# A fused adaLN attention and MLP block: weight loads queued behind the first keys' stores, key block loads between them, and one accumulator in another PSUM bank

## The chip, the core and the metric

The kernel runs on one core of a Trainium2 chip. The metric is device time in microseconds (us) of one launch. The engines that matter here are TensorE (PE, matrix products into the eight PSUM banks), VectorE (DVE), ScalarE (ACT), GpSimd (POOL) and SyncE (SP), which issues all of the DMA transfers in one queue, in program order. Each engine executes its own instructions in order; a semaphore makes one wait for another.

## What is computed

```
h  = layernorm(x) * (1 + ca) + sa                 # x: 2048 x 512
q, k, v = split(h @ wqkv)                          # 32 heads of width 16
o  = softmax(q k^T / 4) v                          # full attention, 2048 keys
x  = x + ga * (o @ wo)
h  = layernorm(x) * (1 + cb) + sb
x  = x + gb * (mish(h @ w1 + b1) @ w2)             # 512 -> 1792 -> 512
# sa, ca, ga, sb, cb, gb = silu(c) @ w_mod, in six parts of 512
```

All of it is fp32. The products are made at the fast rate of a rounded format: each operand is split into a high part and a low part, and three products (high-high, high-low, low-high) are summed in PSUM.

## The kernel before

The order of nearly all work is written out by hand. The program has four stages.

**Start** (lines 337 to 555). x and the first weight slices come in, the layer norm and its transposes are made per block of 512 rows (`tb` = 0 to 3), and the first unit of keys is made for each block, with the first unit of queries beside block 0. Such a unit (`qk_unit`) is 12 products of 128x512 into one PSUM bank; ACT rounds the bank to `qh`, DVE subtracts to `ql` (line 95), and SP stores both to the scratch tensor `kscr` in HBM (lines 284 and 285). From there `load_k` (line 330) loads the block back, 16 rows a head spread to three 16-row groups, into `ka0` and `ka1`, the two key tiles of the first head group. A bank is either one of the ring (`ring`, six banks, four in this stage) or one of the two separate banks `ms` and `acc`.

**Lead-in** (steps t = -20 to -1). Softmax needs the row maximum first. `max_pair` (line 587) makes two products of queries and keys into two neighbouring ring banks (line 595), and DVE reduces the pair to its maxima (line 597); there are 40 pairs, 32 of the first head group (`n` = 0: eight for each of the four key blocks, block by block), and 8 of the second. Beside each pair three or four slots of dense work run on PE (line 133): the rest of the q, k and v units, in *couples* of accumulators in the banks `ring` 4, `ring` 5, `ms` and `acc` in turn. When such a unit is finished, ACT copies its bank away (line 270 for queries and keys as `qf`, line 299 for values as `vq`), and for `qf` POOL makes `qh` and `ql`.

The units use weight slices. The list `plan` names them: its entry 0 is a unit of queries, entry 1 the value units, entries 2 and 3 key units. A slice comes by one DMA into the tile `wr` (line 233; there is one buffer), ACT rounds it to `wh` (line 88), and POOL subtracts to `wl` (line 95), which frees `wr`. The slice of entry i + 3 is loaded after the last unit of entry i, at a *hook*: `at(h, f)` runs f at half step h = 2t, so h fixes the place in the program and not a time.

In the same stage the first six of 32 weight blocks of the later MLP are prepared (`early_prep`, line 1565): a load of 256 KB into the tile `ep` (line 1570), a split on POOL (lines 92 and 95, seven half steps later), and two stores to `w1scr` (line 1578, three half steps after that). They start at the half steps -37, -34, ..., -22.

**Attention with the MLP beside it** (t = 0 to 511). Each step makes scores, their exponentials on ACT (line 639), the product with v (line 654), and the maxima of the head group after next (lines 581 and 583). The MLP of a finished block of rows runs in the gaps of PE.

**Tail.** The last block's output projection and MLP.

The maxima of the first head group must be in the query tiles before the first scores: `neg_max` (line 605), `max_rows` (line 614, a transpose on PE at line 616, then `mh` on ACT and `mt` on DVE), and four small DMAs `qa<-mt` (line 625).

DMAs are counted on eight semaphores in turn, so a DMA isn't issued before the eighth one ahead of it has landed.

Of the kernel before, what the change touches and what calls it, by code (L numbers as in the profile page):

```python
# [18 lines left out]
def adaln_block(ctx: ExitStack, tc: tile.TileContext, x, wqkv, wo, w1, b1, w2, c, w_mod, out):  # L19
# [9 lines left out]
    NB = S // TB  # L29
# [9 lines left out]
    PRO = 16 + LEAD  # L39
# [4 lines left out]
    LATE_LOAD = {4: -4, 5: 9}  # L44
# [41 lines left out]
    def hi_copy(eng, hi, src):  # L86
        if eng == "a":
            nc.scalar.copy(hi, src)
        elif eng == "v":
            nc.vector.tensor_copy(hi, src)  # L90
        else:
            nc.gpsimd.tensor_scalar(hi, src, 1.0, 0.0, op0=ALU.mult, op1=ALU.add)

    def lo_sub(eng, lo, src, hi):
        (nc.gpsimd if eng == "p" else nc.vector).tensor_sub(lo, src, hi.bitcast(F32))  # L95
# [15 lines left out]
    def mm3(acc, ah, al, bh, bl, late="a"):  # L111

        n = len(ah)
        seq = ((ah, bh), (ah, bl), (al, bh)) if late == "a" else ((ah, bh), (al, bh), (ah, bl))
        seq = [(l[k], r[k]) for l, r in seq for k in range(n)]
        for i, (l, r) in enumerate(seq):
            mm(acc, l, r, i == 0, i == len(seq) - 1)
# [42 lines left out]
    def bank(tag="ms"):  # L160
        if not isinstance(tag, str):
            return tag
        return ring() if tag == "ring" else ps.tile([P, TB], F32, tag=tag, name="bk", bufs=1)
# [39 lines left out]
    def at(h, f):  # L203

        hooks.setdefault(h, []).append(f)
# [23 lines left out]
    def slice_load(kind, i, pool=None, lp=None):  # L229
        w = P if kind < 2 else 2 * P  # L230
        raw = (pool or qp).tile([P, DK, w], F32, tag="raw" if pool is pw else "wr", name="wr", bufs=2 if lp else 1)
        o = kind * D + i * w
        nc.sync.dma_start(raw, wqkv[:, o:o + w].rearrange("(k p) m -> p k m", p=P))
        slices[kind, i] = raw
# [10 lines left out]
    def qk_unit(kind, ct, tb, tag):  # L245

        wh, wl = slices[kind, ct]
        acc = bank(tag)
        ts_ = slice(tb * TB, (tb + 1) * TB)
        mm3(acc, [wh[:, k, :] for k in range(DK)], [wl[:, k, :] for k in range(DK)],  # L250
            [h_h[:, k, ts_] for k in range(DK)], [h_l[:, k, ts_] for k in range(DK)], "b")

        def fin(h=None):
            late = h is not None and -4 <= h < 3
            if late and not spares:
                for v in range(2):
                    both = ap.tile([P, DK, TB], F32R, tag=f"o_{v}", name="late", bufs=1)
                    spares.extend(both[:, i, :] for i in range(DK))
            if late:
                qh, ql = spares.pop(), spares.pop()  # L260
            else:
                qh = qp.tile([P, TB], F32R, tag="qh", name="qh", bufs=2)
                ql = qp.tile([P, TB], F32R, tag="ql", name="ql", bufs=2)
            if h is None:
                hi_copy("a", qh, acc)
                lo_sub("v", ql, acc, qh)
            else:
                qf = (ap.tile([P, TB], F32, tag=f"p{len(spares) // 2 % 2 * 2}", name="qf", bufs=3) if late else
                      pw.tile([P, TB], F32, tag="raw", name="qf", bufs=1))
                nc.scalar.copy(qf, acc)  # L270
                hi_copy("p", qh, qf)
                lo_sub("p", ql, qf, qh)
            scr, rows = (qscr, 50) if kind == 0 else (kscr, 48)

            def put():
                put_away.add((kind, ct, tb))
                o = 8 * ct * rows * S + tb * TB
                if kind == 0:
                    for r, src in enumerate((qh, qh, ql)):
                        nc.sync.dma_start(dap(scr, o + r * S, [[rows * S, 8], [3 * S, DH], [1, TB]]), src.bitcast(F32))  # L280
                    return
                hi = qh.bitcast(F32)
                twice = bass.AP(tensor=hi.tensor, offset=hi.offset, ap=[list(hi.ap)[0], [0, 2], [1, TB]])
                nc.sync.dma_start(dap(scr, o, [[3 * S, P], [2 * S, 2], [1, TB]]), twice)
                nc.sync.dma_start(dap(scr, o + S, [[3 * S, P], [1, TB]]), ql.bitcast(F32))

            put() if h is None else at(clear(h + (5 if h > 60 else 2)), put)
        return fin
# [34 lines left out]
    def load_k(pp, tb=None):  # L323
        n, j = divmod(pp, 2)
        h = 4 * (n % G) + 2 * j
        kt = ka[pp % NR].bitcast(F32)
        at_ = slice(0, S) if tb is None else slice(tb * TB, (tb + 1) * TB)
        assert {(1, h // 8, i) for i in (range(NB) if tb is None else (tb,))} <= put_away, (pp, put_away)
        for s in range(2):
            nc.sync.dma_start(kt[64 * s:64 * s + 48, at_], kscr[h + s, :, at_])  # L330
# [6 lines left out]
    with ExitStack() as es:  # L337
# [185 lines left out]
        for tb in range(NB):  # L523
            if tb + 2 < NB:
                stats_tb(tb + 2)
            parts = []
            early = []
            for kind in (1, 0) if tb == 0 else (1,):
                fin = qk_unit(kind, 0, tb, "ring")
                parts.append((pe_queue[2 * DK:], fin))  # L530
                early.append(pe_queue[:2 * DK])
                pe_queue.clear()
            if tb == 0:
                (kw, qw) = early
                early = [[m for k in range(DK) for m in (kw[k], qw[k], kw[DK + k])], qw[DK:]]
            pe_queue.extend(m for e in early for m in e)
            pe_run()
            if tb in (1, 2):
                for kc in (2 * tb - 2, 2 * tb - 1):
                    unit(v_unit(0, kc, "ring"))  # L540
            if tb + 1 < NB:
                tr_tb(tb + 1, CUT1)
            for late, fin in parts:
                pe_queue.extend(late)
                unit(fin)
            if tb + 1 < NB:
                tr_tb(tb + 1, CUT2)
            if tb + 2 < NB:
                apply_tb(tb + 2)
            if tb == 0:  # L550
                for pp in range(2):
                    load_q(pp, 48)
            for pp in range(2):
                load_k(pp, tb)
        slice_split(0, 1)


# [534 lines left out]
    _, w1s, w2s, wos = state[last]  # L1092
# [407 lines left out]
    def do_specials(h):  # L1500
        if specials and h >= specials[0][0]():
# [5 lines left out]
    plan = [(-PRO, 0, 1, (0,)), (-PRO, 2, 0, range(4, 16)), (-PRO, 1, 1, range(NB)), (-PRO, 1, 2, range(NB)),  # L1507
            (-PRO, 0, 2, (0,)), (0, 2, 1, range(16)), (0, 1, 3, range(NB)), (0, 0, 3, (0,))]
# [3 lines left out]
    def planned(i, a, tag):  # L1512
        _, kind, sl, args = plan[i]
        unit = v_unit(sl, a, tag) if kind == 2 else qk_unit(kind, sl, a, tag)

        def fin(h):
            if a == args[-1]:
                if i + 2 < len(plan):
                    d = 4 if h > 0 else 1
                    split_at[i + 2] = LATE_SPLIT.get(i + 2, h + d)  # L1520
                    split = lambda: slice_split(*plan[i + 2][1:3], hi_eng="p" if h > 0 else "a")
                    split() if h < -4 else at(split_at[i + 2], split)
                if i + 3 < len(plan):
                    at(LATE_LOAD.get(i + 3, h + 7), lambda: slice_load(*plan[i + 3][1:3]))
            unit(h)
            if (kind, sl, a) == (2, 0, NKC - 1):
                at(max(0, h + 2), lambda: first_mods(max(0, h + 2)))
            if i + 1 == len(plan) and a == args[-1]:
                mst["qkv"] = h // 2 + 3
        return fin  # L1530

    at(-2 * PRO, lambda: slice_load(*plan[2][1:3]))
    order = (3, 4, 2, 5)

    def first_mods(h, j=0):
# [26 lines left out]

    EARLY = 6

    def early_prep(i, h):

        scr, src, _ = preps[i]
        lo, hi = [ap.tile([P, TB], F32R, tag=f"p{(1, 3, 0, 2)[i % 4]}", name="ep", bufs=4 - i % 4 // 2) for _ in range(2)]
        raw = lo.bitcast(F32)
        nc.sync.dma_start(raw.rearrange("p (k m) -> p k m", m=P), src)  # L1570

        def split():
            hi_copy("p", hi, raw)
            lo_sub("p", lo, raw, hi)

        def put():
            for v, part in enumerate((hi, lo)):
                nc.sync.dma_start(scr[:, v, :], part.bitcast(F32))

        at(h + 7, split)  # L1580
        at(h + 10, put)

    for i in range(EARLY):
        at(3 * i - 37, lambda i=i: early_prep(i, 3 * i - 37))

    def start_preps(h, i=EARLY, turn=0, puts=()):

# [75 lines left out]
```

## Time and profile before

| | |
|---|---|
| median of 3 runs | 1693.15 us (1690.56, 1694.89, 1693.15) |
| the profiled execution | 1691.93 us |
| its span, first to last instruction | 1690.1 us |
| mean granted TensorE clock | 0.996 of full speed |
| DVE busy over the span | 1431.6 us (85%) |
| ACT busy over the span | 1357.3 us (80%) |
| POOL busy over the span | 812.5 us (48%) |
| moved by DMA | 239.02 MB, mean 141 GB/s |

A busy time is the sum over an engine's instructions in the named stretch. In the time line a row gives start, duration, engine, line, operation, output and inputs, and in brackets the idle time just before it on its engine with what ended that. In the table by stretches a row gives busy time and instruction count of PE, of its weight loads, DVE, ACT and POOL, then the granted TensorE clock (1.00 is full speed), the busy share of the DMA engines and what they moved. All that the change touches lies in the first 104 us, the start and the lead-in.

### The profile page before, as it was taken

To read this page: it belongs to the slowest core of one execution; us is meant where nothing else is said; L and a number is where in the kernel's file an instruction comes from. 1 tells how busy PE (TensorE), PEld (TensorE's weight loads), DVE (VectorE), ACT (ScalarE), POOL (GpSimd) and SP (SyncE) were. 2 spreads that over 40 slices of the span, in tenths; PEclk is the share of its full clock that TensorE was granted. 3 is DMA by queue.
4 is the path that set the end of the run, shared out by engine and by line. 5 is a ranking of instruction groups with operands and counts; after the bars stand their busy time and mean duration, and the time that the engine had idled before them with its cause. 6 is when DMAs were issued, how large, how long until landed. Compare 5 with 4: busy or idle time off the path is not lost.

```text
span 1690.1 us, 34360 instructions
## 1 busy us (share of the span) xinstructions
PE 1667.0 (99%) x12707; PEld 932.1 (55%) x12707; DVE 1431.6 (85%) x2372; ACT 1357.3 (80%) x2618; POOL 812.5 (48%) x839
## 2 busy tenths in 40 slices
PE   8989999999999999999999999999999999999999
PEld 6855665555444455555555455555555455555687
DVE  6978888888989888888889888888889888883377
ACT  7157777777778988888888998888888998889674
POOL 5556224655313564556323565556323565555442
PEclk9999999999999999999999999999999999999999
DMA  7777556777755433434355434534354433534161
GB/s 261 218 272 200 147 147 188 222 222 216 230 146 143 113 95 93 121 88 129 85 137 152 115 77 93 141 76 126 87 145 122 130 94 81 144 103 131 76 228 63
DMA packets 114984, 239.02 MB, mean 141 GB/s; under 512 B 24500, under 2 KB 50120, under 8 KB 108864
## 3 DMA queue, kind: packets, MB, share of 16 engines
q1 hardware_dynamic: 114808, 236.82, 49.5%
q8 instruction: 100, 1.64, 0.4%
q14 instruction: 68, 0.56, 0.1%
q10 hardware_dynamic: 8, 0.00, 0.0%
HBM read 180.48 MB, written 51.45 MB: 137 GB/s over the span
## 4 chain that ended last, share of the span: by engine, by line
PE 89%; DVE 4%; DMA 3%; ACT 2%; issue 1%; SPq 0%; POOL 0%; ACTq 0%; DVEq 0%; POOLq 0%
PE bk L654 29%; PE ring L636 22%; PE ring L581 19%; PE bk L133 11%; PE ring L1267 2%; PE ring L126 2%; DVE mx L583 2%; ACT pr L639 1%; PE bk L126 1%; DVE mx L597 1%; PE ring L133 1%; DMA ka<-kscr 1%; DMA kscr<-qh 0%; DMA qa<-mt 0%; PE ring L970 0%
## 5 line engine op out<-in xcount | busy, mean ns | idle before, releaser
L583 DVE TENSOR_REDUCE mx<-ring 128x1 f32<-128x512 f32 x1968 | 1221.9, 681 | 151.1 <-PE ring L581 136.6
L639 ACT ACTIVATE pr<-ring 128x512 f32<-128x512 f32 x2048 | 1078.5, 603 | 207.5 <-PE bk L133 122.7
L581 PE MATMUL ring<-ka,qa 64*128 64x512 f32 x1968 | 817.8, 429 | 1.2 <-ACT pr L639 1.0
L636 PE MATMUL ring<-qa,ka 64*128 64x512 f32 x2048 | 759.1, 402 | 3.4 <-ACT pr L639 1.9
L654 PE MATMUL bk<-pr,vg 128*32 128x512 f32 x4096 | 545.1, 604 | 0.0
L581 PEld LDWEIGHTS ring<-ka,qa 64*128 64x128 f32 x1968 | 350.6, 184 | 326.2 <-DVE mx L583 251.4
L636 PEld LDWEIGHTS ring<-qa,ka 64*128 64x128 f32 x2048 | 373.8, 184 | 192.3 <-DVE mx L583 113.2
L133 PE MATMUL bk<-h,w 64*128 64x512 f32 (+1 forms) x1080 | 277.9, 390 | 0.0
L133 PE MATMUL bk<-w,a_h 64*128 64x512 f32 x632 | 211.1, 413 | 0.0
L133 PEld LDWEIGHTS bk<-h,w 64*128 64x128 f32 x1080 | 178.6, 185 | 10.0 <-ACT pr L639 1.5
L654 PEld LDWEIGHTS bk<-pr,vg 128*32 128x32 f32 x4096 | 81.3, 108 | 135.6 <-issue 126.4
L133 PE MATMUL bk<-w,a_l 64*128 64x512 f32 x316 | 124.3, 393 | 0.0
L133 PEld LDWEIGHTS bk<-w,a_h 64*128 64x128 f32 x632 | 106.8, 184 | 3.0 <-ACT hb L848 0.8
L1026 POOL TENSOR_TENSOR y<-yd,y 128x512 f32<-128x512 f32 x44 | 56.9, 1292 | 88.9 <-ACT yd L1025 79.5
L860 POOL TENSOR_SCALAR qq<-ee 128x512 f32<-128x512 f32 x25 | 15.5, 621 | 169.1 <-ACT ee L854 169.1
L876 POOL TENSOR_TENSOR qq<-qq,rr 128x512 f32<-128x512 f32 x42 | 54.2, 1289 | 85.7 <-ACT rr L870 85.7
L862 POOL TENSOR_TENSOR hb<-hb,ee 128x512 f32<-128x512 f32 x42 | 54.1, 1288 | 79.7 <-DVE ee L858 77.7
L133 PE MATMUL bk<-w,o_hl 64*128 64x512 f32 x288 | 79.3, 405 | 0.0
L95 POOL TENSOR_TENSOR a_l<-hb,a_h 128x512 fp32r<-128x512 f32 x53 | 73.1, 1379 | 4.4
L133 PE MATMUL bk<-h_h,wl 64*128 64x512 f32 x192 | 63.3, 426 | 0.3 <-ACT pr L639 0.3
L133 PEld LDWEIGHTS bk<-w,a_l 64*128 64x128 f32 x316 | 58.3, 185 | 3.1
L133 PE MATMUL bk<-h_h,wh 64*128 64x512 f32 x192 | 53.9, 413 | 5.1 <-ACT vq L299 4.8
(226 smaller groups left out, 1902.6 us busy)
## 6 DMA issues: line engine op xcount, KB each, us to landing
ka<-kscr SPq DMA_DIRECT2D x124, 384.0 KB
w<-w2scr SPq DMA_DIRECT2D x56, 512.0 KB
w<-w1scr SPq DMA_DIRECT2D x46, 512.0 KB
vg<-vscr SPq DMA_DIRECT2D x32, 552.0 KB
qa<-qscr SPq DMA_DIRECT2D x124, 100.0 KB
qscr<-qh SPq DMA_DIRECT2D x32, 256.0 KB
w2scr<-hl SPq DMA_DIRECT2D x14, 512.0 KB
kscr<-qh SPq DMA_DIRECT2D x12, 512.0 KB
```

Of the source, the lines that this page charges most:

```text
L95: (nc.gpsimd if eng == "p" else nc.vector).tensor_sub(lo, src, hi.bitcast(F32))
L126: nc.tensor.matmul(acc, l, r, start=start, stop=stop)
L133: i = nc.tensor.matmul(acc, l[64 * g:64 * g + 64], r[64 * g:64 * g + 64], start=start and not then, stop=bool(stop and then))
L581: nc.tensor.matmul(pm, qt[64 * s:64 * s + 64, qs * P:(qs + 1) * P], kt[64 * s:64 * s + 64, kb * TB:(kb + 1) * TB], start=True, stop=True)
L583: nc.vector.tensor_reduce(out=mxs[n][:, s, 4 * j + qs, kb:kb + 1], in_=pm, op=ALU.max, axis=AX.X)
L636: nc.tensor.matmul(p_, kt[64 * s:64 * s + 64, kc * P:(kc + 1) * P], qt[64 * s:64 * s + 64, :], start=True, stop=True)
L639: e = nc.scalar.activation(pr, p_, AF.Exp, scale=SCALE)
L654: nc.tensor.matmul(accs[n][32 * h:32 * h + 32, :], vgs[n][:, o:o + 32], pts.pop((t, h)), start=(kc == 0), stop=(kc == 15))
L862: (nc.vector if tail else nc.gpsimd).tensor_mul(hb, hb, ee)
L876: nc.gpsimd.tensor_mul(qq, qq, rr)
L1026: nc.gpsimd.tensor_add(y[i], yd, y[i])
L1267: nc.tensor.matmul(po[i // 2][:, i % 2, :], l[:, s], w[:, r, :], start=(f == 0 and j == 0), stop=(f == FT - 1 and j == 2))
```

## The change

The change has three parts. The loads of six MLP blocks are taken out of `early_prep` and put into `first_loads`, which runs at the first half step of the lead-in, together with the load of the slice of entry 2; their splits and stores get places of their own. The loads of key blocks 2 and 3 leave the start and go between those loads. The unit of keys of the last block (`tb` = 3) is summed in the bank `ms`. Besides, a slice that follows a unit finished before half step -20 (entry 3 alone) is loaded two half steps after that unit, where it was seven.

```diff
             for kind in (1, 0) if tb == 0 else (1,):
-                fin = qk_unit(kind, 0, tb, "ring")
+                fin = qk_unit(kind, 0, tb, "ring" if tb + 1 < NB else "ms")
...
             for pp in range(2):
-                load_k(pp, tb)
+                if tb < 2:
+                    load_k(pp, tb)
...
-                    at(LATE_LOAD.get(i + 3, h + 7), lambda: slice_load(*plan[i + 3][1:3]))
+                    at(h + 2 if h < -20 else LATE_LOAD.get(i + 3, h + 7), lambda: slice_load(*plan[i + 3][1:3]))
...
-    at(-2 * PRO, lambda: slice_load(*plan[2][1:3]))
+    def first_loads():
+        slice_load(*plan[2][1:3])
+        for i in range(EARLY):
+            early_load(i)
+            if i % 2:
+                for pp in range(2):
+                    if i < 4:
+                        load_k(pp, 2 + i // 2)
+
+    at(-2 * PRO, first_loads)
...
-    def early_prep(i, h):
+    raws = {}
+
+    def early_load(i):
 
         scr, src, _ = preps[i]
         lo, hi = [ap.tile([P, TB], F32R, tag=f"p{(1, 3, 0, 2)[i % 4]}", name="ep", bufs=4 - i % 4 // 2) for _ in range(2)]
         raw = lo.bitcast(F32)
         nc.sync.dma_start(raw.rearrange("p (k m) -> p k m", m=P), src)
+        raws[i] = scr, raw, hi, lo
+
+    def early_prep(i, h):
...
-        at(h + 7, split)
-        at(h + 10, put)
+        at(h, split)
+        at(h + 3, put)
 
     for i in range(EARLY):
-        at(3 * i - 37, lambda i=i: early_prep(i, 3 * i - 37))
+        early_prep(i, (-38, -36, -34, -32, -27, -25)[i])
```

The lines behind the first edit have other numbers in the changed program: 1570 is 1582, 1578 is 1595, 561 is 562, 595 is 596.

On SP, at the end of the start, the program before has, from the stores of key block 2 on (`kscr<-qh` and `kscr<-ql` are the stores of a key block, `ka_98` and `ka_99` the two key tiles of the first head group, `ep` the MLP blocks):

```order
L284 DMA kscr<-qh 128x2x512
L285 DMA kscr<-ql 128x512
L330 DMA ka_98<-kscr 48x512 x2
L330 DMA ka_99<-kscr 48x512 x2
L284 DMA kscr<-qh 128x2x512
L285 DMA kscr<-ql 128x512
L330 DMA ka_98<-kscr 48x512 x2
L330 DMA ka_99<-kscr 48x512 x2
L233 DMA wr<-in_A_wqkv 128x4x128
L1570 DMA ep<-in_B_w 128x4x128 x4
L1578 DMA w1scr<-ep 128x512 x2
```

and the changed program, from the same stores on:

```order
L284 DMA kscr<-qh 128x2x512
L285 DMA kscr<-ql 128x512
L284 DMA kscr<-qh 128x2x512
L285 DMA kscr<-ql 128x512
L233 DMA wr<-in_A_wqkv 128x4x128
L1582 DMA ep<-in_B_w 128x4x128 x2
L330 DMA ka_98<-kscr 48x512 x2
L330 DMA ka_99<-kscr 48x512 x2
L1582 DMA ep<-in_B_w 128x4x128 x2
L330 DMA ka_98<-kscr 48x512 x2
L330 DMA ka_99<-kscr 48x512 x2
L1582 DMA ep<-in_B_w 128x4x128 x2
```

The stores of key block 3 and the slice of entry 2 no longer stand behind the loads of key block 2, and all six `ep` loads stand ahead of the first store to `w1scr`.

On SP, a little later, around the load of the slice of entry 3 (the `wr` row; `qscr<-qh` and `qscr<-ql` store the query unit of entry 0, `vscr<-vq` values, `qa_102` and `ka_700` belong to the second head group), before:

```order
L280 DMA qscr<-ql 8x16x512
L1570 DMA ep<-in_B_w 128x4x128
L1578 DMA w1scr<-ep 128x512 x2
L306 DMA vscr<-vq 128x4x272
L1570 DMA ep<-in_B_w 128x4x128
L321 DMA qa_102<-qscr 50x512 x2
L330 DMA ka_700<-kscr 48x2048 x2
L1578 DMA w1scr<-ep 128x512 x2
L233 DMA wr<-in_A_wqkv 128x4x128
L1578 DMA w1scr<-ep 128x512 x4
```

and in the changed program (the tile `ka_700` is called `ka_693` there):

```order
L1595 DMA w1scr<-ep 128x512 x8
L233 DMA wr<-in_A_wqkv 128x4x128
L280 DMA qscr<-qh 8x16x512 x2
L280 DMA qscr<-ql 8x16x512
L1595 DMA w1scr<-ep 128x512 x2
L306 DMA vscr<-vq 128x4x272
L1595 DMA w1scr<-ep 128x512 x2
L321 DMA qa_102<-qscr 50x512 x2
L330 DMA ka_693<-kscr 48x2048 x2
```

The slice of entry 3 is now ahead of the query unit's stores, of the first value store of the lead-in and of the second head group's loads, and behind eight stores to `w1scr`.

On POOL the splits of the blocks (`ep`) and of the slice of entry 2 (`wl`) stand like this before:

```order
L561 MEMSET ka_702 128x2048
L92 TENSOR_SCALAR ep<-ep 128x512
L95 TENSOR_TENSOR ep<-ep 128x512
L95 TENSOR_TENSOR wl<-wr,wh 128x512
L92 TENSOR_SCALAR qh<-qf 128x512
L95 TENSOR_TENSOR ql<-qf,qh 128x512
```

and in the changed program:

```order
L562 MEMSET ka_695 128x2048
L92 TENSOR_SCALAR ep<-ep 128x512
L95 TENSOR_TENSOR ep<-ep 128x512
L92 TENSOR_SCALAR ep<-ep 128x512
L95 TENSOR_TENSOR ep<-ep 128x512
L92 TENSOR_SCALAR ep<-ep 128x512
L95 TENSOR_TENSOR ep<-ep 128x512
L92 TENSOR_SCALAR ep<-ep 128x512
L95 TENSOR_TENSOR ep<-ep 128x512
L95 TENSOR_TENSOR wl<-wr,wh 128x512
L92 TENSOR_SCALAR qh<-qf 128x512
L95 TENSOR_TENSOR ql<-qf,qh 128x512
```

The slice's split stands behind four block splits, where it stood behind one. PE, DVE and ACT keep their order; there only the bank of one key unit is another.

More of the change, by code (lines that the diff above doesn't have):

```diff
@@ L1570, in early_prep @@
         nc.sync.dma_start(raw.rearrange("p (k m) -> p k m", m=P), src)
+        raws[i] = scr, raw, hi, lo
+    def early_prep(i, h):
         def split():
+            scr, raw, hi, lo = raws[i]
             hi_copy("p", hi, raw)
@@ L1576, in put @@
         def put():
+            scr, _, hi, lo = raws.pop(i)
             for v, part in enumerate((hi, lo)):
                 nc.sync.dma_start(scr[:, v, :], part.bitcast(F32))
-        at(h + 7, split)
-        at(h + 10, put)
+        at(h, split)
+        at(h + 3, put)
     for i in range(EARLY):
-        at(3 * i - 37, lambda i=i: early_prep(i, 3 * i - 37))
+        early_prep(i, (-38, -36, -34, -32, -27, -25)[i])
     def start_preps(h, i=EARLY, turn=0, puts=()):
```

## The prediction

> **What bounds the kernel now.** I began with the table of stretches, because the share over the whole span hides where PE waits.
>
> ```profile
> 46.00:48.00 2.00, 0.84 (x3) 0.37 (x2) 0.75 (x2) 0.92 (x2) 0.16 (x1) 1.00 0.84 281
> 50.00:52.00 2.00, 2.00 (x16) 2.00 (x15) 1.51 (x2) 0.00 (x0) 2.00 (x2) 0.50 0.35 131
> 84.00:88.60 4.60, 0.00 (x0) 0.00 (x0) 1.35 (x2) 0.88 (x3) 0.18 (x1) 0.76 1.05 361
> 88.60:93.20 4.60, 4.53 (x21) 3.49 (x23) 1.80 (x4) 0.66 (x3) 2.95 (x3) 0.50 1.10 393
> 110.00:1690.00 1580.00, 1570.79 (x11876) 852.18 (x11875) 1345.02 (x2249) 1308.92 (x2534) 754.95 (x753) 1.00 0.48 133
> ```
>
> From 110 us to the end PE is busy 1570.79 of 1580 us, DVE 1345 and ACT 1309. The change moves nothing there, so what the lead-in gains or loses goes through to the end one for one. In the lead-in there are two holes: PE is busy 0.84 of 2 us at 46 to 48, and not at all from 84 to 88.6. After each the granted clock is down to 0.50. The time line of DVE shows what the holes cost, since DVE's 40 pair reductions set the pace between them.
>
> ```profile
> 47.70 0.69 DVE L95 TENSOR_TENSOR ql<-ring,qh 128x512 fp32r<-128x512 f32 x1 [1.25 <-ACT qh L88]
> 49.06 1.23 DVE L597 TENSOR_REDUCE mx<-ring 128x2 f32<-128x1024 f32 x1 [0.67 <-PE ring L595]
> 50.77 1.23 DVE L597 TENSOR_REDUCE mx<-ring 128x2 f32<-128x1024 f32 x1 [0.48 <-PE ring L595]
> 52.46 32.89 DVE L597 TENSOR_REDUCE mx<-ring 128x2 f32<-128x1024 f32 x29 [0.47 <-PE ring L595]
> 91.26 1.23 DVE L597 TENSOR_REDUCE mx<-ring 128x2 f32<-128x1024 f32 x1 [5.91 <-PE ring L595]
> 92.52 0.34 DVE L610 TENSOR_REDUCE mm<-mx 128x16 f32<-128x64 f32 x2
> 92.97 2.42 DVE L597 TENSOR_REDUCE mx<-ring 128x2 f32<-128x1024 f32 x2
> 95.30 0.33 DVE L619 SCALAR_TENSOR_TENSOR mt<-mh,lows,ring 32x128 fp32r<-32x128 f32 x1
> 95.99 7.01 DVE L597 TENSOR_REDUCE mx<-ring 128x2 f32<-128x1024 f32 x6 [0.35 <-PE ring L595]
> ```
>
> 29 reductions run without a gap in 32.89 us, 1.134 us each. DVE is idle for 0.67, 0.48, 0.47 and 5.91 us, each time for PE. The waits and the rows of PE and ACT say why PE was late:
>
> ```profile
> ACT wh L88 <- DMA wr<-in_A_wqkv: 7.1, 1, 7.1
> PE bk L133 <- ACT vq L299: 4.8, 1, 4.8
> 46.22 0.78 PE L126 MATMUL ring<-h_l,wh 128*128 128x512 f32 x2 [0.16 <-POOL h_l L479]
> 48.44 0.58 PE L595 MATMUL ring<-ka,qa 64*128 64x512 f32 x2 [1.44 <-DVE ql L95]
> 103.05 0.49 PE L636 MATMUL ring<-qa,ka 64*128 64x512 f32 x1 [0.43 <-DVE mx L597]
> 80.25 0.37 ACT L299 COPY vq<-bk 128x256 f32<-128x256 f32 x1 [2.32 <-PE bk L133]
> 87.72 0.62 ACT L88 CAST wh<-wr 128x512 fp32r<-128x512 f32 x1 [7.10 <-DMA wr<-in_A_wqkv]
> 88.25 0.37 ACT L299 COPY vq<-bk 128x256 f32<-128x256 f32 x1
> ```
>
> At 84 us PE needs the accumulator that ACT empties at 88.25. ACT had been ready since 80.62, but the rounding of the weight slice of entry 3 stands ahead of that copy, and the slice landed only at 87.7. At 47 us the first pair waits for `ql`, because the last key unit sits in a ring bank that the pair needs. At 103.05 the first scores of attention wait for DVE: the lead-in ends when its reductions end.
>
> **The change, part by part.** *The bank.* With the unit in `ms`, the first pair no longer waits for `ql`. PE can issue it when its last unit product has been issued, two products of about 0.22 us after 46.22, at 46.7 instead of 48.44. DVE still makes `ql` first, until 48.39, so the first reduction starts there and not at 49.06: 0.67 us. The unit itself must now wait until `ms` is free of the last transposes. DVE's row for that bank, before the unit's fourth product waits for ACT anyway, is
>
> ```profile
> 42.31 0.75 DVE L474 SCALAR_TENSOR_TENSOR hf<-bk,modc,h_h 128x512 f32<-128x512 f32 x1
> 44.16 0.50 PE L126 MATMUL ring<-h_h,wh 128*128 128x512 f32 x1 [0.18 <-ACT h_h L473]
> ```
>
> so three products start at 43.06 and are through by 43.7, before the fourth can start at 44.16. It costs nothing; without that cover it would be 0.3 us.
>
> *The idle times behind the first two reductions* (0.48 and 0.47) come from a PE at half clock: the first three reductions start 1.71 and 1.69 us apart, since the pairs come no faster. PE now leads by two pairs when DVE starts, so both idle times go, 0.95 us, if the clock holds. Bounds 0 and 0.95; I take 0.95, with the other end as a rival.
>
> *The slice of entry 3.* When is it issued and when needed? SP and POOL rows of before:
>
> ```profile
> 46.97 0.98 SPq L285 DMA_DIRECT2D kscr<-ql  x1
> 51.33 1.71 SPq L330 DMA_DIRECT2D ka<-kscr  x4
> 59.61 2.09 SPq L1570 DMA_DIRECT2D ep<-in_B_w  x4
> 73.75 0.80 SPq L1570 DMA_DIRECT2D ep<-in_B_w  x1
> 76.38 0.78 SPq L330 DMA_DIRECT2D ka<-kscr  x2
> 79.00 0.38 SPq L233 DMA_DIRECT2D wr<-in_A_wqkv  x1
> 49.48 5.29 POOL L561 MEMSET ka<- 128x2048 f32 x3
> 63.42 0.63 POOL L92 TENSOR_SCALAR ep<-ep 128x512 fp32r<-128x512 f32 x1 [8.65 <-DMA ep<-in_B_w]
> 65.37 1.29 POOL L95 TENSOR_TENSOR wl<-wr,wh 128x512 fp32r<-128x512 f32 x1
> 79.79 0.62 POOL L92 TENSOR_SCALAR ep<-ep 128x512 fp32r<-128x512 f32 x1 [1.80 <-DMA ep<-in_B_w]
> ```
>
> An `ep` load took 3.8 us where SP was idle ahead of it (59.61 to 63.42), 6.0 us in traffic (73.75 to 79.79), and the slice 8.7 us (79.00 to 87.72). In the changed program key block 3 is stored right after `ql` (48.4), the slice of entry 2 and two `ep` loads go out by about 50 us, key block 2 still at some 51.3 when its stores have landed, two more `ep` loads by 54. POOL is free at 54.77 (49.48 + 5.29) and needs 1.95 us a block (63.42 to 65.37): four blocks end at 62.6 if the loads take 4 to 6 us, and `wl` of entry 2 at 63.9, against 66.66 before. That frees the one `wr` buffer, the eight `w1scr` stores have been issued meanwhile, and the slice of entry 3 goes out at 64 instead of 79. At 8.7 us it lands at 72.7. ACT reaches it behind the copy of 80.25, which everything above moves 1.6 us forward, at 79.0. The slack is 6 us, so the wait of 7.1 us is gone, and ACT empties the bank at about 80, where PE wants it at 82.
>
> What is late next there? DVE: from 85.35 on it needs the pairs, and PE's spacing of pairs in that part is a hair above DVE's:
>
> ```profile
> 81.15 0.43 PE L595 MATMUL ring<-ka,qa 64*128 64x512 f32 x2
> 82.30 0.44 PE L595 MATMUL ring<-ka,qa 64*128 64x512 f32 x2
> ```
>
> 1.15 against 1.134 us, 0.15 us over the nine pairs that are left. So DVE's idle time of 5.91 us goes, with the half clock of 88.6 to 93.2 inside it. The 0.35 us before 95.99 stays: PE's transpose of the maxima lies there.
>
> *The loads of key blocks 2 and 3.* Moving them is needed to let the stores and early loads pass; block 2 is used by the 17th pair (48.4 + 16 x 1.134 = 66.5) and lands before 60, block 3 eight pairs later. They cost nothing, with 6 us of cover. *The `ep` work* is the same twelve POOL instructions and eighteen DMAs, earlier. *The second head group's keys* (76.38 above) follow at about 72 and are wanted at 85.
>
> Sum: 0.67 + 0.95 + 5.91 = 7.53 us, less 0.15 for PE's spacing, 7.4 us. From the other side: DVE's work from 48.39 on, 1.23 + 1.23 + 32.89 + 1.23 + 0.34 + 2.42 + 0.33 + 7.01 = 46.7, with 0.35 idle, ends at 95.4 instead of 103.0. The profiled execution took 1691.93 us (span 1690.1), 1.2 under the median of the three runs, 1693.15; off the median the forecast is 1685.7 us.
>
> [...] PE idled only 1.6 us around 46 to 48 (0.16 and 1.44), and the clock was at 0.50 by 50 us. In the changed program PE runs ahead by two pairs and then waits for the first reduction's end (48.39 + 1.23), from about 48.5 to 49.6 (an estimate, at 0.9 us a pair with three slots, a little under the 1.15 us of a pair with four): 1.1 us in the same place. Whether that is short enough no row shows. [...]
>
> **Rivals.**
> 1. *The clock falls anyway* at the first pairs. PE again takes 1.7 us for a pair of three slots while DVE takes 1.134, and the two idle times, 0.95 us, stay: 1686.6 us. For it: the 1.1 us above.
> 2. *A transfer on the way into attention takes over.* The maxima must reach the query tiles before the first scores, and on SP their four DMAs stand behind the load of v, which waits for the last value store:
>
> ```profile
> 88.64 0.37 SPq L306 DMA_DIRECT2D vscr<-vq  x1
> 95.08 0.33 SPq L568 DMA_DIRECT2D vg<-vscr  x1
> 95.71 2.86 SPq L625 DMA_DIRECT2D qa<-mt  x4
> ```
>
> That store took 6.4 us. It now starts at about 80 and `mt` is ready at 88, so 8 us are left. With traffic squeezed into less time it could take 11; then the scores come 3 us late: 1688.7 us. Against it: the way from `mt` to the scores (7.4 us) does not shrink.
> 3. *The slice still comes late,* because SP is one queue and the slice now waits for POOL's four splits and eight stores. Then ACT waits as before and only 1.6 us are won: 1691.5 us. It needs the slice 6 us later than reckoned.
> 4. *Slower: `wl` of entry 2 holds PE up.* It now stands behind four block splits on POOL, and PE's first product with it comes at
>
> ```profile
> 70.08 0.39 PE L133 MATMUL bk<-h_h,wl 64*128 64x512 f32 x1
> ```
>
> or 68.5 after the gain at the start. Each microsecond that the fourth `ep` load lands after 65.3 (68.5 - 1.95 - 1.29) stops PE, and DVE two pairs later. At 8.7 us for each step in turn (key store, `ep` load) it lands at 67: a loss of 2 of the 7.4. Slower than before begins when it lands after 72.7, 18 us after its issue; at 20 us, twice the longest seen, 1695 us. Against it: it is 256 KB, and the stretch of 50 to 52 us moved only 131 GB/s.
>
> **Chances.** Forecast 0.55, the clock 0.25, the late maxima 0.09, the late slice 0.06, slower 0.05. The three runs of before differ by 4 us, so the median of a new kernel may lie 2 us off. The range of 8 in 10 is 1681.8 to 1690: below, the forecast with that scatter and another microsecond and a half of PE's half clock that I count as hidden; above, the late maxima with some scatter. About 0.3% (5.1 us) is what a measurement of this kernel can tell from no change. The forecast passes it by 2.3 us and the clock rival by 1.5, so faster by more than that gets 0.74 (0.9 of the first, 0.85 of the second, little of the third), within it 0.20, and slower 0.06.
>
> **What would show it.** The first `mx` starts within 0.1 us of the end of `ql`, and PE's row ahead of the first pair names no wait for `ql`. The load of `wr` for entry 3 is issued near 64 us and no row says that ACT's `wh` waited for it; PE has no stretch without work between 80 and 90 us, and the clock stays at 1.00 there. DVE's largest idle time in the lead-in falls below 0.5 us, and the first scores start near 95.5 us. After that PE's busy time differs by less than 1 us. I am wrong if the first scores come later than 98 us, or if a wait of PE for `wl` or for a DMA appears in the lead-in.

## The result and the profile after

The changed kernel took 1687.83 us (median of 8 runs, 1684.32 to 1689.62) and the kernel before, on the same chip, 1693.05 us (8 runs, 1690.56 to 1697.11). The ratio is 0.9969, with a 95% interval of 0.9958 to 0.9979: 5.2 us faster, where the forecast was 7.4. The profiled execution took 1687.18 us, with a span of 1685.4.

The table of stretches of the changed kernel, with the columns and stretches shown of before:

```profile
46.00:48.00 2.00, 1.25 (x5) 0.56 (x4) 0.74 (x2) 0.94 (x2) 0.13 (x1) 1.00 0.50 141
50.00:52.00 2.00, 2.00 (x28) 1.92 (x25) 2.00 (x3) 0.00 (x0) 2.00 (x2) 1.00 1.04 380
84.00:88.60 4.60, 2.07 (x15) 1.78 (x16) 2.07 (x4) 0.16 (x1) 0.00 (x0) 1.00 1.05 301
88.60:93.20 4.60, 3.98 (x34) 2.85 (x32) 4.25 (x6) 0.43 (x2) 0.00 (x0) 1.00 1.02 260
```

PE's clock is 1.00 in all four, and the hole at 84 us is smaller but still there: PE is busy 2.07 of 4.60 us. The time line of DVE, and three of PE's rows that name a wait:

```profile
47.67 0.69 DVE L95 TENSOR_TENSOR ql<-bk,qh 128x512 fp32r<-128x512 f32 x1 [1.26 <-ACT qh L88]
48.28 36.34 DVE L598 TENSOR_REDUCE mx<-ring 128x2 f32<-128x1024 f32 x32
87.50 2.36 DVE L598 TENSOR_REDUCE mx<-ring 128x2 f32<-128x1024 f32 x2 [2.50 <-PE ring L596]
90.45 7.02 DVE L598 TENSOR_REDUCE mx<-ring 128x2 f32<-128x1024 f32 x6 [0.35 <-PE ring L596]
```

```profile
86.04 0.46 PE L596 MATMUL ring<-ka,qa 64*128 64x512 f32 x1 [2.40 <-DMA ka<-kscr]
86.99 0.47 PE L596 MATMUL ring<-ka,qa 64*128 64x512 f32 x1 [0.48 <-DMA ka<-kscr]
97.52 0.50 PE L637 MATMUL ring<-qa,ka 64*128 64x512 f32 x1 [0.43 <-DVE mx L598]
```

All 32 reductions of the first head group now run from the end of `ql` on without a gap. Then DVE is idle for 2.50 us, because PE waits for the two key tiles of the *second* head group (`ka<-kscr`). The first scores start at 97.52 instead of 103.05. The old wait is gone; this is ACT's rounding of the slice of entry 3, without a bracket, so ACT did not wait:

```profile
78.65 0.62 ACT L88 CAST wh<-wr 128x512 fp32r<-128x512 f32 x1
```

DVE's idle times after `ql` were 0.67 + 0.48 + 0.47 + 5.91 + 0.35 = 7.88 us and are now 2.50 + 0.35 = 2.85. That is 5.0 of the 5.5 us; the rest is DVE's own rows, packed a little closer (36.34 us for 32 reductions, which took 36.58). After the first scores, the span is 1587.1 us before and 1587.9 now, so nothing more was won there.

Why the keys came late stands on SP and POOL:

```profile
47.71 0.45 SPq L284 DMA_DIRECT2D kscr<-qh  x1
48.22 0.88 SPq L285 DMA_DIRECT2D kscr<-ql  x1
49.14 1.23 SPq L284 DMA_DIRECT2D kscr<-qh  x1
50.47 1.18 SPq L285 DMA_DIRECT2D kscr<-ql  x1
51.69 1.21 SPq L233 DMA_DIRECT2D wr<-in_A_wqkv  x1
53.03 1.57 SPq L1582 DMA_DIRECT2D ep<-in_B_w  x2
62.22 5.54 SPq L1595 DMA_DIRECT2D w1scr<-ep  x8
68.00 0.63 SPq L233 DMA_DIRECT2D wr<-in_A_wqkv  x1
70.94 3.31 SPq L1595 DMA_DIRECT2D w1scr<-ep  x2
75.36 2.03 SPq L1595 DMA_DIRECT2D w1scr<-ep  x2
79.12 0.77 SPq L330 DMA_DIRECT2D ka<-kscr  x2
```

```profile
58.74 0.63 POOL L92 TENSOR_SCALAR ep<-ep 128x512 fp32r<-128x512 f32 x1 [3.99 <-DMA ep<-in_B_w]
66.60 1.29 POOL L95 TENSOR_TENSOR wl<-wr,wh 128x512 fp32r<-128x512 f32 x1
```

Read them as one chain. SP issues without a pause from 47.71 on, but four of its issues take 0.88 to 1.23 us and not 0.4, so the first `ep` loads go out at 53.03 and not by 50. They land at 58.7, POOL waits 3.99 us for them, `wl` of entry 2 ends at 67.89, and the slice of entry 3 goes out at 68.00 where the forecast had 64. From there to the second head group's keys it is 11.1 us where the forecast had 8. Issued from 79.12 on, the two key tiles land at about 86 and 87; PE wanted the first at 83.6 (86.04 less 2.40).

### The profile page after: what moved, and what is told of

Its sections match the earlier page's. It is cut to its first block, busy times and chain, and to the rows that moved or that the text cites. A ratio compares the mean times of both kernels' runs of the same rounds, so it can differ in the third digit from the quotient of the medians.

```text
span 1685.4 us, 34363 instructions
## 1 busy us (share of the span) xinstructions
PE 1664.2 (99%) x12707; PEld 928.9 (55%) x12707; DVE 1431.5 (85%) x2372; ACT 1357.4 (81%) x2618; POOL 812.5 (48%) x839
## 4 chain that ended last, share of the span: by engine, by line
PE 90%; DVE 4%; DMA 2%; ACT 2%; issue 1%; SPq 0%; POOL 0%; ACTq 0%; DVEq 0%; POOLq 0%
PE bk L655 29%; PE ring L637 22%; PE ring L582 19%; PE bk L133 12%; PE ring L1268 2%; PE ring L126 2%; DVE mx L598 1%; ACT pr L640 1%; PE bk L126 1%; DVE mx L584 1%; DMA ka<-kscr 1%; DMA wr<-in_A_wqkv 1%; DMA xt<-in_A_x 0%; PE ring L133 0%; PE ring L971 0%
## 5 line engine op out<-in xcount | busy, mean ns | idle before, releaser
L879 POOL TENSOR_TENSOR rr<-rr,qq 128x512 f32<-128x512 f32 x42 | 54.1, 1289 | 3.5
```

The lines of the kernel that those rows point to most:

```text
L879: nc.gpsimd.tensor_mul(rr, rr, qq)
```

## The experiments

Every version computes the whole result. The ratios are to the kernel before, run beside each version on the same chip; its medians were 1693.03 (21 runs), 1693.18 (16) and 1693.48 us (9).

| version | median us (range) | ratio, 95% interval | first scores, us |
|---|---|---|---|
| changed, again | 1686.36 (1686.15 to 1691.03) | 0.9963, 0.9949 to 0.9976 | 97.75 |
| changed, third time | 1685.07 (1684.45 to 1688.15) | 0.9959, 0.9947 to 0.9972 | 95.71 |
| before + slice hook alone | 1694.65 (1690.04 to 1697.80) | 1.0004, 0.9994 to 1.0013 | 103.05 |
| before + bank alone | 1695.45 (1692.18 to 1698.50) | 1.0011, 1.0002 to 1.0020 | 105.58 |
| changed without the bank | 1686.53 (1685.41 to 1688.31) | 0.9954, 0.9940 to 0.9967 | 97.33 |
| changed without the hook | 1691.51 (1689.83 to 1696.12) | 0.9989, 0.9980 to 0.9999 | 103.41 |
| changed, `ep` loads at old places | 1689.95 (1685.99 to 1692.32) | 0.9972, 0.9959 to 0.9986 | 97.97 |
| the same, load of v later | 1687.32 (1684.34 to 1689.70) | 0.9967, 0.9954 to 0.9979 | 96.22 |
| changed, keys early | 1684.91 (1684.54 to 1689.37) | 0.9954, 0.9941 to 0.9967 | 95.11 |
| the same, second time | 1685.12 (1683.57 to 1689.76) | 0.9959, 0.9945 to 0.9973 | 95.37 |
| keys early, without the bank | 1684.85 (1684.67 to 1686.50) | 0.9945, 0.9933 to 0.9958 | 96.88 |
| keys early, load of v later | 1683.94 (1683.16 to 1685.63) | 0.9949, 0.9936 to 0.9961 | 94.91 |

The last column comes from one profiled execution of each, and the scatter of the start is in it: `ql` of the last key block begins between 47.1 and 48.8 us.

**The slice hook alone.** The kernel before, with one edit:

```diff
-                    at(LATE_LOAD.get(i + 3, h + 7), lambda: slice_load(*plan[i + 3][1:3]))
+                    at(h + 2 if h < -20 else LATE_LOAD.get(i + 3, h + 7), lambda: slice_load(*plan[i + 3][1:3]))
```

> The kernel before with one edit: the slice of entry 3 is loaded two half steps after its unit, not seven. Theory (the late slice was nearly the whole loss): it is issued at about 67 us in place of 79, ACT no longer waits for it, the start of the lead-in stays as before (DVE idle 0.67, 0.48, 0.47), the keys of the second head group come in time since the start is later, and the first scores start at 97.1 us, as early as in the changed kernel: 1687.3 us. Rival (the early queue is needed to have slice and keys in time): ACT or PE waits 2 us or more for one of them, the first scores come after 99 us, and the time is 1689 us or more.

It is no faster. The stall at 84 us is gone, and yet PE's first scores wait elsewhere. Rows of PE, ACT, DVE and SP:

```profile
64.75 0.62 ACT L88 CAST wh<-wr 128x512 fp32r<-128x512 f32 x1 [5.70 <-DMA wr<-in_A_wqkv]
68.71 1.23 DVE L597 TENSOR_REDUCE mx<-ring 128x2 f32<-128x1024 f32 x1 [3.06 <-PE ring L595]
92.26 7.01 DVE L597 TENSOR_REDUCE mx<-ring 128x2 f32<-128x1024 f32 x6 [0.35 <-PE ring L595]
96.82 2.79 SPq L625 DMA_DIRECT2D qa<-mt  x4
103.05 0.76 PE L636 MATMUL ring<-qa,ka 64*128 64x512 f32 x1 [4.14 <-DMA qa<-mt]
```

DVE is through at 99.3, but the transfers of the maxima went out only at 96.8, and PE waits 4.14 us for them: the end that rival 2 named. The wait costs more than its length. This row of the stretches, just behind it, shows the clock at 0.50:

```profile
104.00:108.00 4.00, 3.71 (x17) 2.55 (x15) 3.20 (x5) 2.25 (x5) 0.00 (x0) 0.50 1.04 369
```

From the first scores on, this execution takes 1590.2 us, where before takes 1587.1. And the slice of entry *2* was late here, which stopped DVE for 3 us. The early queue puts that slice ahead of eight key loads; in the version with that queue but without the hook, below, ACT does not wait for it. So the rival of this expectation came.

**The bank alone.** The kernel before, with one edit:

```diff
-                fin = qk_unit(kind, 0, tb, "ring")
+                fin = qk_unit(kind, 0, tb, "ring" if tb + 1 < NB else "ms")
```

> The kernel before with one edit: the last key unit is summed in the separate bank. Theory (the slice's landing is set by SP and POOL and not by PE, so a start won by PE is waited away at 84 us): DVE's first three idle times go, 1.6 us, the one behind the slice grows from 5.9 to 7.5 us, the first scores stay at 103 us, and the time at 1693 us. Rival (the two holes add up): the first scores start at 101.4 us and the time is 1691.4 us.

```profile
48.29 17.10 DVE L597 TENSOR_REDUCE mx<-ring 128x2 f32<-128x1024 f32 x15
71.06 1.23 DVE L597 TENSOR_REDUCE mx<-ring 128x2 f32<-128x1024 f32 x1 [5.67 <-PE ring L595]
93.57 1.23 DVE L597 TENSOR_REDUCE mx<-ring 128x2 f32<-128x1024 f32 x1 [2.88 <-PE ring L595]
```

Time line of DVE: the start gains what was reckoned, no idle time in the first fifteen reductions, and then DVE waits it away at both slices (5.67 us at entry 2, 2.88 at entry 3). The slice of entry 2 went out at 62.33, behind the key loads, where the profile of before has it at 59.07, so a part of this is SP's own scatter. Neither expectation had the stall at entry 2; with it the first scores came at 105.58 us. A start that is 1.6 us earlier buys nothing while a transfer with its own time stands behind it.

**The bank undone**, in the changed kernel: the same edit backwards.

> The changed kernel with the last key unit in the ring again. Theory (in the changed kernel the lead-in's end is set by the second head group's keys and the maxima's transfers, so the start won by the bank is waited away): DVE's first idle times come back (0.7, and up to 0.95 if the clock falls), the wait for the keys at 83 us shrinks by as much, first scores at 97.5 to 98.2 us, time within 0.5 us of the changed kernel's 1686.4. Rival (the two add up): first scores at 99.1 us, 1688 us.

Rows of DVE and of the stretches:

```profile
48.92 36.30 DVE L598 TENSOR_REDUCE mx<-ring 128x2 f32<-128x1024 f32 x32 [0.67 <-PE ring L596]
50.00:52.00 2.00, 2.00 (x25) 1.89 (x23) 2.00 (x3) 0.00 (x0) 2.00 (x2) 1.00 1.03 383
```

The first 0.67 us are lost again, but the clock holds and the two idle times behind do not return; then PE waits for the keys less (0.61 and 0.70 us). The time is that of the changed kernel (1686.53 us here; 1685.07 to 1687.83 in its three comparisons). In the changed kernel as it stands the bank is worth nothing that can be measured.

**The hook undone**, in the changed kernel: the hook edit backwards.

> The changed kernel with the slice of entry 3 seven half steps after its unit again, which puts it behind the second head group's keys on SP. Theory (one queue: what goes first lands first): the slice is issued at 78 to 80 us and lands at 85 to 87, ACT holds back the value copy, PE stops from about 82.5 to 87 us; the keys are issued 1 us earlier and are no longer waited for; the two waits overlap, so the first scores start at 97.5 to 98.5 us, and the time is within 1 us of the changed kernel's 1686.4. Rival (the hook is what counts): first scores at 100 us or later, 1689 us or more.

Rows of SP, ACT and DVE:

```profile
78.24 0.77 SPq L330 DMA_DIRECT2D ka<-kscr  x2
79.06 0.42 SPq L233 DMA_DIRECT2D wr<-in_A_wqkv  x1
87.49 0.62 ACT L88 CAST wh<-wr 128x512 fp32r<-128x512 f32 x1 [7.61 <-DMA wr<-in_A_wqkv]
91.03 1.23 DVE L598 TENSOR_REDUCE mx<-ring 128x2 f32<-128x1024 f32 x1 [6.42 <-PE ring L596]
```

At its old hook the slice is issued behind the second head group's keys at 79.06, lands at 87.5 as before, and the old stall is back whole: the rival, and not the expected 97.5 to 98.5 us. The early queue and the bank alone are worth 1.7 us (1693.18 less 1691.51), the hook alone nothing, both together 5 to 8. They are not two gains to be added: the hook makes slice 3 early, and the early queue keeps slice 2 and what stands behind on SP from taking its place.

**The early `ep` loads undone.** The changed kernel with the six `ep` loads, splits and stores at the half steps of before; the slice of entry 2 still ahead of the key loads:

```diff
-        for i in range(EARLY):
-            early_load(i)
...
+        for tb in (2, 3):
+            for pp in range(2):
+                load_k(pp, tb)
...
-        at(h, split)
-        at(h + 3, put)
+        at(h, lambda: early_load(i))
+        at(h + 7, split)
+        at(h + 10, put)
...
-        early_prep(i, (-38, -36, -34, -32, -27, -25)[i])
+        early_prep(i, 3 * i - 37)
```

> The changed kernel with the six MLP block loads put back at their old places; the slice of entry 2 still goes out ahead of the key block loads, the slice of entry 3 two half steps after its unit, the bank stays. Theory (the early block loads are needed, since otherwise the MLP stores are still in the queue when attention is to start): no wait for a slice at 67 or 84 us, but the last MLP stores go out at 80 to 88 us ahead of the last value store, so the maxima's transfers are late and the first scores wait 3 us or more for them, at 100 us or later; 1689 to 1691 us. Rival (only the two slices mattered): first scores at 97.7 us or earlier, 1686.4 us or less.

Rows of DVE, SP and PE:

```profile
47.72 36.35 DVE L598 TENSOR_REDUCE mx<-ring 128x2 f32<-128x1024 f32 x32
86.62 0.33 DVE L620 SCALAR_TENSOR_TENSOR mt<-mh,lows,ring 32x128 fp32r<-32x128 f32 x1
81.86 1.03 SPq L1592 DMA_DIRECT2D w1scr<-ep  x2
90.56 2.93 SPq L626 DMA_DIRECT2D qa<-mt  x4
97.97 0.76 PE L637 MATMUL ring<-qa,ka 64*128 64x512 f32 x1 [4.02 <-DMA qa<-mt]
```

DVE is idle only for the 0.36 us ahead of its last six reductions, as the forecast had it for the whole change. But with the last `w1scr` stores at 82 us the last value store is issued at 83, the load of v behind it holds SP until 90.13, and the transfers of the maxima, ready at 87, go out at 90.56. PE's wait of 4.02 us is again followed by the low clock:

```profile
100.00:104.00 4.00, 3.71 (x19) 2.42 (x17) 2.79 (x5) 2.25 (x5) 0.00 (x0) 0.50 1.04 393
```

So the profiled span is 2.8 us longer than that of the changed kernel (1688.2 and 1685.4 us), although the first scores come only 0.45 us later. The early `ep` work is only in part what takes the maxima's transfers off the path: with it the load of v went out at 90.16, 89.40 and 87.85 us in the three profiles of the changed kernel, and in the first two the late keys had made the maxima ready only at 90.1 and 89.4. It is the same early `ep` work that delays the keys.

**Its load of v two half steps later**, behind the maxima's transfers:

```diff
-    at(-7, lambda: load_v(0))
+    at(-5, lambda: load_v(0))
```

> This is the version whose early weight loads stay at their old places, with one more edit: the load of the first value block is issued two units later, so that it no longer stands on SP's queue ahead of the transfers of the first maxima. Theory (in the run without this edit the maxima were ready at 86.6 us and their transfers were issued at 90.6 only because SP stood at the load of v, which waits for the last value store): the transfers are issued at about 88, TensorE's wait for them at the first scores shrinks from 4.0 to about 1 us, the first scores come at 95 to 95.5, and the time is 1687 us. Rival (the transfers themselves are slow beside the weight traffic): the wait stays at 3 to 4 us, the first scores at 97.5 to 98 and the time at 1690 us.

The transfers went out at 88.48, PE waited 1.92 us and not 4.02, and the first scores came at 96.22. The queue was about half of the wait; the four transfers themselves took longer (3.61 us on SP against 2.93), which is a part the theory left out. With a wait of 1.92 us the clock stayed at 1.00. The profiled execution is the fastest of the five.

**The changed kernel twice more.**

> The changed kernel once more, as the measure for the runs beside it: 1687.8 us, first scores at 97.5 us, PE waiting 2.4 and 0.5 us for the keys of the second head group. If that wait is an accident of one profile, it is under 1 us here.

> The changed kernel again, for the comparison with the version with early keys: 1686.4 to 1687.8 us, first scores at 97.5 to 97.8, and a wait of TensorE for the keys of the second head group of 0.5 to 2.5 us near 86 us. If the spread between chips is larger than the difference sought, its median lies outside that range.

The third profile has the lead-in that was forecast. Its rows of SP, POOL, DVE and PE:

```profile
51.14 1.74 SPq L1582 DMA_DIRECT2D ep<-in_B_w  x2
66.07 0.69 SPq L233 DMA_DIRECT2D wr<-in_A_wqkv  x1
77.56 0.77 SPq L330 DMA_DIRECT2D ka<-kscr  x2
55.43 0.63 POOL L92 TENSOR_SCALAR ep<-ep 128x512 fp32r<-128x512 f32 x1
85.46 2.34 DVE L598 TENSOR_REDUCE mx<-ring 128x2 f32<-128x1024 f32 x2
95.71 0.46 PE L637 MATMUL ring<-qa,ka 64*128 64x512 f32 x1 [0.67 <-DMA qa<-mt]
```

SP reached the `ep` loads at 51.1 and not 53.0, POOL did not wait for the first of them, the keys went out 1.6 us earlier, and DVE has no idle time before 85.46. The span is 1682.7 us, 7.4 less than that of before. In the second profile the `ep` loads went out at 52.4, POOL waited 2.86 us, PE 1.39 and 0.77 us ahead of the first two products with the second head group's keys (the trace puts the first of these waits down to DVE, the second to the keys) and 1.36 for the maxima's transfers; DVE was idle for 1.78 us. So the wait was no accident of one profile, and the step stands on an edge: a difference of 2 us in when SP gets to the loads goes with keys that are late or in time. I had expected a wait for the keys of 0.5 to 2.5 us in the third one too; it has none.

**The second head group's keys early.** The changed kernel with their loads at the end of the first loads:

```diff
+        load_pair(2)
...
-    for pp, h in ((2, -22), (3, -10)):
+    for pp, h in ((3, -10),):
```

> The changed kernel with the loads of the second head group's queries and keys taken ahead of the first MLP store. Theory (the rest of the gain is lost because these loads stand on SP behind twelve MLP stores): PE's wait for them is gone, DVE's idle time of 2.50 us falls under 0.3, the first scores start at 94.9 us, and the time is 2.5 us under the changed kernel, 1685.3 us. Rival (the transfers as a whole are the limit, so another one is late instead): the weight slice of entry 3, the value load or the maxima's four small transfers hold PE or DVE up, the first scores stay at 97 to 98 us, and the time stays at 1687.8 us.

> The version with the second head group's keys loaded at once, again, beside the changed kernel on the same chip. Theory: it stays 1.5 to 2.5 us ahead of the changed kernel, 1684.9 against 1686.4 to 1687.8 us, with the first scores at 95.1 against 97.6. Rival (the 1.5 us seen before came from the spread of the runs): the medians are within 0.5 us of each other, although the first scores stay apart.

Rows of SP, DVE and PE (first of the two):

```profile
62.00 0.78 SPq L330 DMA_DIRECT2D ka<-kscr  x2
85.09 2.35 DVE L598 TENSOR_REDUCE mx<-ring 128x2 f32<-128x1024 f32 x2
95.11 0.50 PE L637 MATMUL ring<-qa,ka 64*128 64x512 f32 x1 [0.43 <-DVE mx L598]
```

The keys go out at 62 instead of 79, DVE is idle nowhere before the maxima, and the first scores wait for DVE alone, at 95.1, where the forecast put them. Against the changed kernel on the same chip the median is 1.45 us lower the first time (1684.91 to 1686.36) and no lower the second (1685.12 to 1685.07), where the changed kernel's profile had no wait for the keys. The expected 1.5 to 2.5 us did not repeat. It removes a wait that some executions have; the intervals of the two ratios overlap both times.

**The same without the bank** (the bank edit backwards):

> The kernel with the second head group's keys loaded early, and the last key unit in the ring again. Theory (with that wait gone DVE is never idle, so now the bank's part shows): DVE's idle times of 0.7 us and up to 0.95 us come back at the start and are made up nowhere, first scores at 95.8 to 96.7 us against 95.1, time 0.7 to 1.6 us above 1684.9. If the clock stays up without the bank, 0.7 us; if it falls, 1.6 us. Rival (transfers set the end there too): first scores at 95.1 us, 1684.9 us.

Stretches and DVE:

```profile
50.00:52.00 2.00, 2.00 (x16) 2.00 (x15) 1.52 (x2) 0.00 (x0) 2.00 (x2) 0.50 1.02 334
49.25 1.23 DVE L598 TENSOR_REDUCE mx<-ring 128x2 f32<-128x1024 f32 x1 [0.79 <-PE ring L596]
```

Here the clock fell to 0.50 at 50 us as in before, DVE lost 0.79, 0.48 and 0.35 us, and the lead-in ended 1.8 us later. The profiled execution is the slowest of the five; the median is the same as with the bank, which was measured on other chips. Whether the bank is worth something once the keys are early stays open.

**Keys early, and the load of v two half steps later:**

> This is the version with the second head group's keys loaded at once behind the first loads, with the load of the first value block issued two units later. Theory (in that version TensorE waits for the maxima themselves, 0.4 us, and not for their transfers): the first scores stay at 95.1, the time stays at 1684.9 us, within 1 us. Rival (the load of v becomes late for the first product with the values, which comes at 102 us): that product waits some 1 to 3 us and the time is 1686 to 1688 us.

The first scores start at 94.91, the first product with v at 101.96 (102.16 without this edit), so v is not late. The median is the lowest of all versions, but its interval overlaps that of the changed kernel. Nor does the lead-in show a gain over keys early alone: from the start of `ql` to the first scores it takes 47.26 us with this edit (47.65 to 94.91) and 47.26 without it (47.85 to 95.11), so the earlier first scores come from an earlier start.

## Why the prediction was right, and where it was not

**Bank, 0.67 us: the mechanism came, its worth did not.** The first reduction starts at the end of `ql`, as reckoned. By itself the bank is 0.11% slower than before (interval 0.02 to 0.20%), and undone in the changed kernel it costs nothing, since other waits take up the time.

**Clock, 0.95 us: came, though not by the way described.** The granted clock at 50 to 52 us is 1.00 in all ten profiled executions with the unit in `ms`, and the idle times are gone in each. With the unit in the ring it fell in two of four. So rival 1 was refuted here. But PE did not lead by two pairs and then wait 1.1 us for a reduction. It issued one pair and waited for ACT's rounding of a slice, in the changed kernel by this row:

```profile
48.21 0.50 PE L133 MATMUL ring<-h_h,wh 64*128 64x512 f32 x1 [0.81 <-ACT wh L88]
```

The pause was made shorter, from 1.44 to 0.81 us, and not only moved; that this cures the clock rests on these counts.

**Slice of entry 3, 5.91 us: right.** The stall is gone with the hook and comes back without it (7.61 us at ACT). Its issue time was off, 66.1 to 68.0 and not 64; the 6 us of slack that the forecast gave took that. One price was misread without harm: the `ep` load of 3.8 us did not follow a pause of SP, which had issued four key loads and a slice right ahead of it; in the changed kernel the first one took 5.7 us (53.03 to 58.74).

**The step that failed** is the sentence that the second head group's keys "follow at about 72 and are wanted at 85". They went out at 77.6 to 79.1. Two terms behind it were mis-sized. The stores, the slice and the `ep` loads were to go out "by about 50 us" at 0.4 us each; the four issues from 48.22 took 0.88 to 1.23, 2.9 us more, and POOL's first block started at 58.74 and not 54.77. And the way from the slice to the keys was taken as 8 us and is 11.1 to 11.5, since four further `w1scr` stores there take SP 5.3 us, after the eight that were counted as issued "meanwhile". Nor were those eight free: in the second and third profile `wl` was ready at 66.78 and 64.89, but the last of the eight was issued only by 67.10 and 65.98, and the slice behind it. The sentence also has no term for the landing. The first key tile came 6.9 us after its issue (79.12 to 86.04), so of the 13 us between 72 and 85 only 4.7 were slack (to PE's need at 83.6), against 7.1 us of delay: the wait of 2.4 us. With the keys issued at 62, and no other edit to the changed kernel, the first scores came at 95.1, where the sum has 95.4: with that wait gone nothing took its place.

**Size.** The changed kernel was 5.2, 6.7 and 8.4 us faster in its three comparisons, the forecast 7.4. In the first profile signs that the forecast gave for itself failed: DVE's largest idle time was 2.50 us and not under 0.5, PE stood still at 84 us, and it waited there for a DMA, which the forecast had named as a sign of being wrong. The shortfall of 2.1 us in the first is about the 2.5 us by which DVE waited in its profile; the third has no such wait. How often an execution has it the runs do not tell.

**Rivals.** The late maxima (rival 2) happen as described, but in the versions with only part of the change: 4.14 us with the hook alone, 4.02 with late `ep` loads. Their price is above the 3 us of the forecast, which left out the clock: from the first scores on these two executions take 1590.2 us, the other twelve 1586.4 to 1588.3. In the three profiles of the changed kernel they cost at most 1.36 us. In the first of them the last value store, issued by 80.9, held the load of v until 90.16, over 9 us and not the 6.4 of before; there the late keys hid it. Rivals 3 and 4 did not come, rival 4 by little: `wl` of entry 2 ended at 67.89, later than the forecast's 63.9, and PE's first product with it started at 68.20, with no wait.

## What to carry to other kernels

When a load is moved forward on a queue that one engine serves, list what is now behind it and give each of those a new time, in issue times measured where the queue runs without a pause into full DMA engines; here the slice that was rescued had 6 us of slack, and the keys behind it, once their landing is counted, under 5. Where one stall hides others a few microseconds long, undo each part in the full change as well as trying it alone: alone, hook and bank were worth nothing. Price a wait of PE with the clock that follows it. If a step ends within 2 us of its need in one profile, take a second and third profile before deciding whether it is late.

## What the runs showed of the hardware

SP's own issue of one DMA is not a fixed cost. A store of `kscr<-qh` took 0.45 us at 47.71 (DMA share 0.50) and 1.23 us at 49.14 (share 1.00 at 48 to 50), and the slice load at 51.69 took 1.21 us (share 1.04 at 50 to 52). The share alone does not decide it: this row of SP in the changed kernel lies in a stretch with a share of 1.05, behind a pause of SP,

```profile
85.97 0.38 SPq L284 DMA_DIRECT2D kscr<-qh  x1
```

and is short. Nor are a full share and the lack of a pause enough: SP issued the two `ep` loads of 61.18 back to back in 0.94 us, with a share of 1.03 at 60 to 62. By the trace's semaphore events a DMA does go out right behind the landing of the eighth one ahead (the slice of entry 3 at 68.00, that landing at 67.94). But a wait for that landing does not explain the four long issues: the DMA eight ahead of each had landed by 44.7, 45.4, 47.4 and 48.5 us, before the issue began (48.22, 49.14, 50.47, 51.69). What holds them the trace does not name.

The clock's fall does not follow the length of a gap alone. In before, 1.44 us of idle PE ahead of the first pair was followed by a granted clock of 0.50; in the changed kernel without the bank the same pause (1.45 us) was followed by 1.00; in the changed kernel PE stood idle for 2.40 us at 84 us and the clock stayed at 1.00 to 93.2. Over the fourteen profiles, between 44 and 130 us, 0.50 followed each of the five pauses of 4.0 us and more (before 4.77, the hook alone 4.14, the bank alone 4.29, the hook undone 5.28, the late `ep` loads 4.02), three of the eleven between 1.2 and 2.7 us (before 1.44, keys early without the bank 1.45, the hook alone 1.97), and none of those under 0.9. In before, the two stretches at 0.50 in that part go from 48.87 to 52.28 us and from 86.42 to 93.24, with 1.00 on both sides. What sets the moment of a fall no run here shows.
